# Output stores of an attention and gated-layers kernel: one store for each group of 32 tokens, issued in turn by SP and ACT

## The chip, the cores and the metric

The kernel runs on one core of a Trainium2 chip. The metric is the device time of one execution in microseconds (us). Traces come from one profiled execution, and times in them count from its first instruction.

## The reference

What is computed, cut to what matters: a Nystrom attention over 4 batches of 8 heads, 576 tokens and 64 values per head, and behind it two gated layers, whose result is the output.

```python
A, Bm, C = sm(q, k_lm), sm(q_lm, k_lm), sm(q_lm, k)     # 32 landmarks per head
# Z: six steps of an iterative pseudo-inverse of Bm
x = (A @ Z @ C @ v)            # to 2304 tokens x 512
x = ((silu(x @ w_gate1) * (x @ w_val1)) @ w_out1)        # d_ff = 1536
out = ((sigmoid(x @ w_gate2) * (x @ w_val2)) @ w_out2)   # 2304 x 512, f32
```

## The kernel before, in words

The attention's factors for each batch b are kept as A transposed (tile AH and its low part) and U = Z C v. The first layer works on U W1 (`uw_steps`): for each of six chunks c of 256 columns of d_ff, and each batch, eight matmuls, one for each head, form U W1 in eight tiles of 32 rows; the matmuls with A follow in `gv1_steps`. Those two functions stay as they are.

The stores belong to the second layer. Its tokens are kept in an order of their own: token number t in batch b is row 576 b + 18 t' + u of the output for t = 32 u + t', so that 32 neighbouring tokens on 32 partitions go to 32 output rows that lie 18 apart. Each row is 512 f32 numbers, 2 KB in one piece.

The second layer runs over d_ff in six chunks c (`NFC`) and in each over five chunks i of tokens: four of 512 tokens (one for each batch, `MT`), and a fifth of 256 tokens, the last 64 of each batch (`NR`). `gv2_steps(c, i)` has two halves ft: gate and value matmuls (tiles pg and pv), sigmoid on ACT (line 491), product on DVE (line 492), and a split into a high and a low part (ACT line 326, DVE line 327). `o2_steps(c, i)` takes 128 tokens at a time (t): six matmuls into a tile po, and DVE adds po to the tile oacc (line 513). In the last chunk (c = 5) the finished oacc tile is stored right behind its add: line 517 for the chunks of 512 tokens, one DMA for each tile of 128 tokens; line 520 for the fifth chunk, two DMAs for each tile. All are issued by SP.

The program interleaves by hand: the first half of the next `gv2_steps` is written ahead of `o2_steps` of the chunk at hand, the second half behind it. In c = 5 the order of the chunks is 0, 1, 2, 4, 3, so chunk 3 (512 tokens) ends the program, with no work behind its last adds but the stores.

The names DMAHW0 to DMAHW7 in the instruction lists are eight completion counters. The program's DMAs take them in turn, and a DMA waits until the DMA that last used its counter, eight DMAs earlier, has landed, unless something else already says so.

Of the kernel before, what the change touches and what calls it, by code (L numbers as in the profile page):

```python
# [14 lines left out]
def nystrom_moe_kernel(tc, q, k, v, wg1, wv1, wo1, wg2, wv2, wo2, out):  # L15
    nc = tc.nc
    B, H, S, D = q.shape
    M = 32
    P = 128
# [8 lines left out]
    MT = 512  # L28
# [14 lines left out]
    def ptile(shape, tag, name):  # L43
        return psum.tile(shape, F32, tag=tag, name=name, bufs=PB[tag])
# [16 lines left out]
    def mm(o, l, r, start=True, stop=True):  # L61
        nc.tensor.matmul(o, l, r, start=start, stop=stop, skip_group_check=True)  # L62
# [314 lines left out]
    def otag(layer, c):  # L377
        nps[0] += 1
        return "oa"[nps[0] % 2] if layer or c >= OA else "o"
# [85 lines left out]
    NR = S - MT  # L465
# [32 lines left out]
    def o2_steps(c, i):  # L498
        w = WO[1, c]
        for t in range(0, CHUNKS[i], P):  # L500
            if c == 0:
                OACC[i, t] = late["o"].tile([P, DM], F32, tag="oacc", name=f"oacc{i}_{t}", bufs=B * S // P)
            acc = OACC[i, t]
            ps = ptile([P, DM], otag(1, c), f"po2_{c}_{i}_{t}")
            n = 0
            for ft in range(2):
                for a, x in TERMS:
                    mm(ps, H2[c, i, ft][a][:, t:t + P], w[:, x, ft, :], start=(n == 0), stop=(n == 5))
                    n += 1
            if c == 0:  # L510
                nc.scalar.copy(acc, ps)
            else:
                nc.vector.tensor_tensor(acc, ps, acc, op=ALU.add)  # L513
            if c == NFC - 1:
                rows = out.rearrange("(b t u) d -> b u t d", b=B, u=L)
                if i < B:
                    nc.sync.dma_start(rows[i, t // M:(t + P) // M], acc)
                else:
                    for x in range(P // NR):
                        nc.sync.dma_start(rows[t // NR + x, MT // M:], acc[NR * x:NR * (x + 1), :])  # L520
            yield


# [81 lines left out]
    for i, (c, b) in enumerate(order):  # L605
        if c + 1 < NFC and b == 0:
            wfill.append(weights(1, c + 1))
        main(g2)
        if i + 1 < len(order):
            nc_, nb_ = order[i + 1]  # L610
            need(1, nc_, 3)
            g2 = gv2_steps(nc_, nb_)
            next(g2)
        need(1, c, 5)
        main(o2_steps(c, b))
# [38 lines left out]
```

## Time and profile before

| | us |
|---|---|
| median of 3 runs | 936.54 |
| lowest, highest | 935.5, 939.15 |
| profiled execution | 937.11 |
| its span, first to last instruction | 935.3 |

The profiled execution is 1.8 us longer than its span, and 0.6 us above the median. Granted TensorE clock over the span: 0.983 of full speed. A page of the profile gives the busy time of each engine, the span in 40 slices, the DMA queues, the chain of work that ended last, and the costliest groups of instructions; the trace behind it can be asked for the instructions of a stretch in order of time and for busy shares in short stretches (the DMA share is the mean over the core's 16 DMA engines).

### The profile page before, as it was taken

What the parts mean: (1) busy time and instruction counts of PE and PEld (TensorE: products, weight loads), DVE (VectorE), ACT (ScalarE), POOL (GpSimd) and SP (SyncE); (2) the same over time, 40 slices, a digit from 0 to 9 for tenths busy, and PEclk for the clock granted to TensorE, in tenths of its full rate; (3) what the DMA queues carried; (4) which work ended last, traced back from release to release, by engine and by line L of the source; (5) the groups of instructions that cost most, each with busy time, mean ns of one, the idle gap of its engine ahead of it and who ended that gap; (6) DMA issues with size and microseconds to landing.
All of it is one profiled execution on the core that took longest, in us unless ns stands there. A gap on an engine that the chain in (4) does not pass through costs nothing.

```text
span 935.3 us, 16158 instructions
## 1 busy us (share of the span) xinstructions
PE 896.4 (96%) x6664; PEld 746.8 (80%) x6664; DVE 549.2 (59%) x1165; ACT 389.7 (42%) x833; POOL 0.7 (0%) x6
## 2 busy tenths in 40 slices
PE   5689999999999999999999999999999999999994
PEld 4456866677989999998998888888888888888883
DVE  7789968647777668869962153455346247232331
ACT  6569745546636346537653262143124114111110
POOL 0000000000000000000000000000000000000000
PEclk9779999999999999999999999999999999999998
DMA  8664311003313103202110021012003000000121
GB/s 271 193 189 151 91 52 39 15 1 91 125 57 90 46 18 119 90 1 91 46 39 7 1 87 49 1 47 88 1 13 123 1 1 23 0 1 1 61 76 67
DMA packets 25617, 57.66 MB, mean 62 GB/s; under 512 B 2760, under 2 KB 5832, under 8 KB 25544
## 3 DMA queue, kind: packets, MB, share of 16 engines
q1 hardware_dynamic: 25544, 56.63, 19.3%
q8 instruction: 52, 0.85, 0.4%
q14 instruction: 21, 0.17, 0.1%
HBM read 51.90 MB, written 4.72 MB: 61 GB/s over the span
## 4 chain that ended last, share of the span: by engine, by line
PE 91%; DVE 5%; ACT 1%; DMA 1%; issue 1%; SPq 0%; ACTq 0%; DVEq 0%
PE po L62 33%; PE pg L62 24%; PE pv L62 23%; PE pu L62 3%; PE nw L62 2%; PE tp L121 2%; DVE lm L107 1%; DMA kin<-in_k_dram 1%; PE cs L62 1%; PE cv L62 1%; PE as L62 1%; PE lt L62 1%; PE et L207 1%; DVE hl L327 0%; DVE cv L295 0%
## 5 line engine op out<-in xcount | busy, mean ns | idle before, releaser
L62 PE MATMUL po<-hh,wo 128*128 128x288 f32 x768 | 162.9, 303 | 1.0 <-DVE uw L327 0.7
L62 PE MATMUL po<-wo,h 128*128 128x512 f32 x648 | 152.2, 390 | 0.0
L492 DVE TENSOR_TENSOR hf<-hf,pv 128x512 f32<-128x512 f32 (+1 forms) x60 | 38.1, 634 | 194.2 <-PE pv L62 194.2
L62 PEld LDWEIGHTS po<-wo,h 128*128 128x128 f32 x648 | 121.1, 188 | 25.4 <-ACT h L326 0.3
L62 PEld LDWEIGHTS po<-hh,wo 128*128 128x128 f32 x768 | 123.0, 188 | 20.6 <-issue 13.7
L62 PE MATMUL pg<-AH,w 128*128 128x512 f32 (+1 forms) x480 | 136.2, 368 | 0.0
L62 PE MATMUL pv<-AH,w 128*128 128x512 f32 (+1 forms) x480 | 136.0, 368 | 0.0
L62 PE MATMUL po<-hl,wo 128*128 128x288 f32 x384 | 115.1, 300 | 0.3 <-DVE hl L327 0.3
L62 PE MATMUL pg<-AH,uw 128*128 128x288 f32 x576 | 98.9, 298 | 2.5 <-ACT uw L326 2.4
L491 ACT ACTIVATE hf<-pg 128x512 f32<-128x512 f32 (+1 forms) x60 | 33.1, 552 | 163.7 <-PE pg L62 163.0
L62 PEld LDWEIGHTS pg<-AH,w 128*128 128x128 f32 x480 | 87.3, 188 | 15.4
L62 PEld LDWEIGHTS pv<-AH,w 128*128 128x128 f32 x480 | 87.0, 189 | 15.0
L62 PE MATMUL pv<-AH,uw 128*128 128x288 f32 x576 | 95.9, 296 | 0.0
L62 PEld LDWEIGHTS pg<-AH,uw 128*128 128x128 f32 x576 | 83.2, 188 | 9.2 <-ACT uw L326 5.3
L326 ACT CAST h<-hf 128x512 fp32r<-128x512 f32 (+1 forms) x60 | 34.6, 576 | 125.6 <-DVE hf L492 125.6
L513 DVE TENSOR_TENSOR oacc<-po,oacc 128x512 f32<-128x512 f32 x90 | 61.9, 691 | 41.1 <-PE po L62 39.9
L62 PEld LDWEIGHTS pv<-AH,uw 128*128 128x128 f32 x576 | 82.6, 188 | 2.9 <-ACT sg L419 0.8
L62 PE MATMUL pg<-x1l,w 128*128 128x512 f32 x192 | 74.7, 389 | 0.0
L62 PE MATMUL pv<-x1l,w 128*128 128x512 f32 x192 | 74.7, 389 | 0.0
L62 PEld LDWEIGHTS po<-hl,wo 128*128 128x128 f32 x384 | 72.2, 188 | 2.7 <-issue 1.1
L447 DVE TENSOR_TENSOR acc<-po,acc 128x288 f32<-128x288 f32 x128 | 55.9, 454 | 16.8 <-PE po L62 16.0
L419 ACT ACTIVATE sg<-pg 128x288 f32<-128x288 f32 x96 | 39.1, 407 | 51.8 <-PE pg L62 51.2
(106 smaller groups left out, 1092.6 us busy)
## 6 DMA issues: line engine op xcount, KB each, us to landing
raw<-in_moe_w_out_dram SPq DMA_DIRECT2D x24, 512.0 KB
raw<-in_moe_w_gate_dram SPq DMA_DIRECT2D x36, 256.0 KB
raw<-in_moe_w_val_dram SPq DMA_DIRECT2D x36, 256.0 KB
kin<-in_k_dram SPq DMA_DIRECT2D x8, 576.0 KB
qin<-in_q_dram SPq DMA_DIRECT2D x8, 576.0 KB
vin<-in_v_dram SPq DMA_DIRECT2D x8, 576.0 KB
out_dram<-oacc SPq DMA_DIRECT2D x16, 256.0 KB
raw<-in_moe_w_gate_dram SPq DMA_DIRECT2D x24, 128.0 KB
```

Of the source, the lines that this page charges most:

```text
L62: nc.tensor.matmul(o, l, r, start=start, stop=stop, skip_group_check=True)
L107: nc.vector.tensor_reduce(lm, src.rearrange("p u d -> p d u"), axis=AX.X, op=ALU.add)
L121: nc.tensor.transpose(ps[:, j], flat(src[:, 2 * u:2 * u + 2]), ident)
L207: nc.tensor.transpose(ps[:, j, :], flat(e[:, r // 2, r % 2]), ident)
L326: nc.scalar.copy(hi, x)
L419: nc.scalar.activation(sg, pss[0], AF.Silu)
L447: nc.vector.tensor_tensor(sl, ps, sl, op=ALU.add)
L491: nc.scalar.activation(h, pss[0], AF.Sigmoid)
L492: nc.vector.tensor_tensor(h, h, pss[1], op=ALU.mult)
L513: nc.vector.tensor_tensor(acc, ps, acc, op=ALU.add)
```

## The change

In place of one store (or two) for each tile of 128 tokens there are four, each of 32 partitions by 512 f32 numbers (64 KB). The even ones are issued by SP, the odd ones by ACT.

```diff
             if c == NFC - 1:
+
                 rows = out.rearrange("(b t u) d -> b u t d", b=B, u=L)
-                if i < B:
-                    nc.sync.dma_start(rows[i, t // M:(t + P) // M], acc)
-                else:
-                    for x in range(P // NR):
-                        nc.sync.dma_start(rows[t // NR + x, MT // M:], acc[NR * x:NR * (x + 1), :])
+                for y in range(P // M):
+                    bb, u = (i, t // M + y) if i < B else ((t + M * y) // NR, (MT + (t + M * y) % NR) // M)
+                    eng = nc.scalar if y % 2 else nc.sync
+                    eng.dma_start(rows[bb, u], acc[M * y:M * y + M, :])
             yield
```

The same rows and bytes are written. The instructions of PE, DVE and POOL keep their order; ACT gets 36 DMAs and SP has 36 in place of 20.

On ACT, in the last chunk of d_ff, the first place is between the split of one half (line 326) and the sigmoid of the next (line 491). Before (h and hf are the tiles of the gated product, the numbers 5_1 are c and i):

```order
L491 ACTIVATE hf_5_0_9510<-pg_5_0_9484 128x512 [waits PE_49,Activation_49]
L326 CAST h_5_0_9513<-hf_5_0_9510 128x512 [waits DVE_49]
L491 ACTIVATE hf_5_1_9543<-pg_5_1_9517 128x512 [waits PE_49,Activation_49]
L326 CAST h_5_1_9546<-hf_5_1_9543 128x512 [waits DVE_49]
L491 ACTIVATE hf_5_1_9612<-pg_5_1_9586 128x512 [waits PE_49,Activation_49]
L326 CAST h_5_1_9615<-hf_5_1_9612 128x512 [waits DVE_49]
```

The same place in the changed kernel:

```order
L326 CAST h_5_1_9546<-hf_5_1_9543 128x512 [waits DVE_49]
L520 DMA out_dram<-oacc_0_6848 32x512 [waits DVE_49]
L520 DMA out_dram<-oacc_0_6848 32x512
L520 DMA out_dram<-oacc_128_6860 32x512 [waits DVE_49]
L520 DMA out_dram<-oacc_128_6860 32x512
L520 DMA out_dram<-oacc_256_6877 32x512 [waits DMAHW0_49,DVE_49]
L520 DMA out_dram<-oacc_256_6877 32x512 [waits DMAHW2_49]
L520 DMA out_dram<-oacc_384_6889 32x512 [waits DMAHW4_49,DVE_49]
L520 DMA out_dram<-oacc_384_6889 32x512 [waits DMAHW6_49]
L491 ACTIVATE hf_5_1_9624<-pg_5_1_9598 128x512 [waits PE_49,Activation_49]
```

Eight DMAs of chunk 0's output now stand ahead of the sigmoid of chunk 1's second half, and they wait for the adds on DVE and for earlier stores.

On SP the other place is the end of the program: the stores of the fifth chunk (oacc_0_7315, oacc_128_7324) and of chunk 3, four tiles of 128 tokens. Before:

```order
L520 DMA out_dram<-oacc_0_7315 2x32x512 [waits DMAHW4_49,DVE_49]
L520 DMA out_dram<-oacc_0_7315 2x32x512 [waits DMAHW5_49]
L520 DMA out_dram<-oacc_128_7324 2x32x512 [waits DMAHW6_49,DVE_49]
L520 DMA out_dram<-oacc_128_7324 2x32x512 [waits DMAHW7_49]
L517 DMA out_dram<-oacc_0_7213 4x32x512 [waits DMAHW0_49,DVE_49]
L517 DMA out_dram<-oacc_128_7222 4x32x512 [waits DMAHW1_49,DVE_49]
L517 DMA out_dram<-oacc_256_7231 4x32x512 [waits DMAHW2_49,DVE_49]
L517 DMA out_dram<-oacc_384_7240 4x32x512 [waits DMAHW3_49,DVE_49]
L649 UNCONDITIONAL_BRANCH
```

In the changed kernel the same end, from the fifth chunk's second tile on:

```order
L520 DMA out_dram<-oacc_128_7324 32x512 [waits DMAHW5_49,DVE_49]
L520 DMA out_dram<-oacc_128_7324 32x512 [waits DMAHW7_49]
L520 DMA out_dram<-oacc_0_7213 32x512 [waits DMAHW1_49,DVE_49]
L520 DMA out_dram<-oacc_0_7213 32x512 [waits DMAHW3_49]
L520 DMA out_dram<-oacc_128_7222 32x512 [waits DMAHW5_49,DVE_49]
L520 DMA out_dram<-oacc_128_7222 32x512 [waits DMAHW7_49]
L520 DMA out_dram<-oacc_256_7231 32x512 [waits DMAHW1_49,DVE_49]
L520 DMA out_dram<-oacc_256_7231 32x512 [waits DMAHW3_49]
L520 DMA out_dram<-oacc_384_7240 32x512 [waits DMAHW5_49,DVE_49]
L520 DMA out_dram<-oacc_384_7240 32x512 [waits DMAHW7_49]
L649 UNCONDITIONAL_BRANCH
```

SP has the odd counters now and ACT the even ones, so that a store waits for the fourth one before it on its own engine: that of the tile two back.

## Rows read from the trace of the kernel before

**Rows 1.** Busy time of each engine over the span, from the page.

```profile
PE 896.4 (96%) x6664; PEld 746.8 (80%) x6664; DVE 549.2 (59%) x1165; ACT 389.7 (42%) x833; POOL 0.7 (0%) x6
```

**Rows 2.** Stretches: busy us (instructions) by engine, granted clock, DMA share, GB/s.

```profile
862.00:922.30 60.30, 59.60 (x285) 49.56 (x283) 22.03 (x34) 8.29 (x15) 0.00 (x0) 1.00 0.18 61
922.30:935.30 13.00, 0.00 (x0) 0.00 (x0) 0.03 (x1) 0.00 (x0) 0.00 (x0) 0.67 0.22 83
```

**Rows 3.** Instructions of DVE and SP at the end, in order of time.

```profile
918.87 1.29 DVE L513 TENSOR_TENSOR oacc<-po,oacc 128x512 f32<-128x512 f32 x2 [0.83 <-PE po L62]
920.26 0.69 DVE L513 TENSOR_TENSOR oacc<-po,oacc 128x512 f32<-128x512 f32 x1
921.63 0.69 DVE L513 TENSOR_TENSOR oacc<-po,oacc 128x512 f32<-128x512 f32 x1 [0.68 <-PE po L62]
...
919.59 4.04 SPq L517 DMA_DIRECT2D out_dram<-oacc  x4
...
922.35 1.27 SPq L517 DMA_DIRECT2D out_dram<-oacc  x1
```

**Rows 4.** What SP's queue waited for: us in total, times, longest.

```profile
SPq L649 <- DMA out_dram<-oacc: 10.6, 1, 10.6
```

**Rows 5.** Short stretches at the end, columns as in rows 2.

```profile
914.00:916.00 2.00, 2.00 (x11) 1.65 (x10) 0.03 (x1) 0.00 (x0) 0.00 (x0) 1.00 0.13 46
...
932.20:932.60 0.40, 0.00 (x0) 0.00 (x0) 0.00 (x0) 0.00 (x0) 0.00 (x0) 0.50 0.26 102
...
933.80:934.20 0.40, 0.00 (x0) 0.00 (x0) 0.00 (x0) 0.00 (x0) 0.00 (x0) 0.50 0.03 10
```

**Rows 6.** SP's issues of stores: duration ns min/median/max, first and last start.

```profile
L517 SPq DMA_DIRECT2D out_dram<-oacc x16: 527/537/1274, 865.9 to 922.4; - x16
L520 SPq DMA_DIRECT2D out_dram<-oacc x4: 511/528/716, 909.8 to 911.7; - x4
```

**Rows 7.** The start of chunk 1's stores: issue on SP, and short stretches.

```profile
882.26 0.53 SPq L517 DMA_DIRECT2D out_dram<-oacc  x1
...
882.80:883.20 0.40, 0.40 (x4) 0.32 (x3) 0.33 (x2) 0.00 (x0) 0.00 (x0) 1.00 0.00 0
883.20:883.60 0.40, 0.40 (x3) 0.33 (x2) 0.39 (x1) 0.00 (x0) 0.00 (x0) 1.00 0.14 31
883.60:884.00 0.40, 0.40 (x3) 0.35 (x2) 0.00 (x0) 0.00 (x0) 0.00 (x0) 1.00 0.40 31
884.00:884.40 0.40, 0.40 (x3) 0.32 (x3) 0.14 (x1) 0.00 (x0) 0.00 (x0) 1.00 0.39 15
884.40:884.80 0.40, 0.40 (x4) 0.32 (x3) 0.40 (x1) 0.00 (x0) 0.00 (x0) 1.00 0.05 5
```

**Rows 8.** A train of four weight loads of 128 KB (64 rows each), last issue and end.

```profile
300.93 0.60 SPq L314 DMA_DIRECT2D raw<-in_moe_w_val_dram  x1
...
301.50:302.00 0.50, 0.50 (x12) 0.34 (x18) 0.50 (x2) 0.50 (x3) 0.00 (x0) 1.00 0.78 217
302.50:303.00 0.50, 0.50 (x17) 0.09 (x1) 0.11 (x1) 0.50 (x2) 0.00 (x0) 1.00 0.62 209
303.00:303.50 0.50, 0.50 (x4) 0.50 (x5) 0.39 (x1) 0.50 (x2) 0.00 (x0) 1.00 0.01 4
```

**Rows 9.** ACT and PE around chunk 0's and chunk 1's stores and at the end.

```profile
872.08 0.60 ACT L491 ACTIVATE hf<-pg 128x512 f32<-128x512 f32 x1 [6.81 <-PE pg L62]
888.40 0.60 ACT L491 ACTIVATE hf<-pg 128x512 f32<-128x512 f32 x1 [6.81 <-PE pg L62]
891.85 0.62 ACT L326 CAST h<-hf 128x512 fp32r<-128x512 f32 x1 [2.86 <-DVE hf L492]
893.73 5.63 PE L62 MATMUL po<-wo,h 128*128 128x512 f32 x24
...
869.30 0.69 DVE L513 TENSOR_TENSOR oacc<-po,oacc 128x512 f32<-128x512 f32 x1 [0.67 <-PE po L62]
913.24 0.60 ACT L491 ACTIVATE hf<-pg 128x512 f32<-128x512 f32 x1 [4.09 <-PE pg L62]
915.97 0.69 DVE L492 TENSOR_TENSOR hf<-hf,pv 128x512 f32<-128x512 f32 x1 [4.82 <-PE pv L62]
```

## The prediction

> **What bounds the kernel now.** I read the page's busy times first: PE is busy for 896.4 of 935.3 us [rows 1]. A change of stores can gain nothing there unless PE waits for one, and no matmul reads what a store writes. So I looked for a stretch in which PE is idle, and the stretches show one: until 922.3 us PE is busy for 59.6 of 60.3 us, and from 922.3 to the end, 13.0 us, no engine computes while the DMA engines run at a share of 0.22 [rows 2]. The reader is to see there that these 13 us are a tail of stores.
>
> The instructions at the end say the same: the last add ends at 921.63 + 0.69 = 922.32, SP issues the last store at 922.35 and is through at 923.62 [rows 3]. Then it waits 10.6 us for the stores to land [rows 4], that is to 934.2, and the last 1.1 us are the end of the program.
>
> What makes the tail long is the rate. While it lasts the DMA share is 0.26 and 102 GB/s flow: 4 of the 16 DMA engines work, at 25 GB/s each [rows 5]. From 914 to 916, where only the fifth chunk's stores are under way, the share is 0.13 at 46 GB/s, 2 engines [rows 5]. The stores' outermost sizes are 4 (4x32x512, line 517) and 2 (2x32x512, line 520). Chunk 3's 1 MB takes 10 us at 102 GB/s, and it starts behind what the fifth chunk's 512 KB left on two of those four engines. Elsewhere more engines work: in a train of loads of 64 rows the share is 0.62 to 0.78, 10 to 12 engines' worth on average, at 209 to 217 GB/s [rows 8].
>
> **The change, part by part.** PE, DVE and POOL keep their order, so until 922.32 nothing should move unless ACT is late (below). What remains is when the last of the new stores lands.
>
> *Rate.* A store is now 32 rows of 2 KB. I take it that its 32 rows go to all 16 engines, two rows each, as those of the 64-row loads go to more than four. Even at the loads' 209 GB/s a tile of 256 KB then needs 1.25 us in place of 2.6, and the 512 KB of the fifth chunk is gone long before chunk 3's first store. The Trainium skill's page "DMA: Bandwidth & Descriptors" (section "Why a DMA increments its semaphore by 16 and not by 1") says that a DMA uses the largest number of engines up to 16 that divides the slowest size of both sides. By that the old stores use 4 and 2, which rows 5 bear out, and the new ones would use 16, which no row here shows.
>
> *Issue.* SP's issues of stores last 0.53 us (median), 0.51 at least; the longest, 1.27 us, is the last one, behind the backlog [rows 6]. I take 0.53 for SP and, lacking any row of an ACT issue, for ACT too. Each engine has two for each tile, side by side with the other.
>
> *Landing time L, from the start of an issue until the counter says so.* From issue to first packet: the issue at 882.26 moves nothing until 883.2 and little before 883.6, about 1.15 us [rows 7]. From last packet to the end of the wait: packets end near 934.0, the wait at 934.2, so 0.2. Between: at full pace two rows of 2 KB on an engine at 25 GB/s take 0.16 us, hence a lower bound L = 1.5. But the first packets of a burst of stores are slow: from 883.2 to 884.8 only 0.4 x (31 + 31 + 15 + 5) = 33 KB pass [rows 7]. If a store of 64 KB pays this start of 1.6 us in full, L = 2.95; if the pair from SP and ACT pay it one after the other, L = 4.55, the upper bound. For small loads the train's last issue starts at 300.93 and its packets are over at about 303.0 [rows 8]: 2.1 + 0.2 gives 2.3. I take L = 2.6, between 2.3 and 2.95.
>
> *The new wait.* A store waits for the fourth one before it on its engine. In the last chunk the adds end at 919.56, about 920.16, 920.95 and 922.32 [rows 3]: the first three tiles come faster than 2 issues of 0.53 allow, so SP's four issues for tiles 0 and 1 start at 919.59, 920.12, 920.65 and 921.18. The third tile's first store must wait for the first tile's to land, 919.59 + L, and so on; the fourth tile's second store starts at 921.18 + L (from L = 2.1 on; below, the issues themselves set it, at 923.30). It lands L later. ACT runs beside it in the same steps.
>
> *Sum.* End of the span = 921.18 + 2 L + 1.1 = 922.28 + 2 L. With L = 2.6 that is 927.5, against 935.3: **7.8 us less**. The bounds: L = 1.5 gives 923.30 + 1.5 + 1.1 = 925.9, 9.4 us less; L = 4.55 gives 931.4, 3.9 us less. Without the wait on the counters the last store would start at 922.88, and the gain with L = 2.6 would be 8.7: the wait gives back about 0.9.
>
> *What is costed at nothing.* SP's 16 more issues: it has nothing else to do there. ACT's 36 issues, 19 us at 0.53, in a stretch where ACT is busy for 8.3 of 60.3 us [rows 2]. They hold up what stands behind them on ACT, which is the sigmoid of the next half. After chunk 0 the last add ends at 869.99 and ACT's two issues are done by 871.1, the sigmoid starts at 872.08 when its matmuls end [rows 9]: covered by 1 us, and by more, since the product also waits for pv. At the program's last sigmoid, 913.24, the fifth chunk's adds (last one done at about 911.15) leave 1 us too, and another 2.1 until the product's own wait for pv ends at 915.97 [rows 9].
>
> Against the profiled execution's 937.11 us this makes 929.3. The median of the runs is 0.57 lower, so for a median I expect 936.54 - 7.8 = 928.7; I give 928.8.
>
> **Rivals.**
>
> *The stores land late.* The queue is then held by its own counters. For: the slow start in rows 7, which 64 KB stores meet more often than 256 KB ones. Against: the loads of 128 KB in rows 8 don't show it. Each us of L costs 2 us at the end. At L = 4.16 the gain falls to 4.7 us, 0.5%, and beyond it the change reads as none: 931.9 to 933.
>
> *The rate stays.* If the small stores still run at 102 GB/s in all, on few engines or one after the other, chunk 3's 1 MB starts at 919.59 + 1.15, pays 1.6, needs 10.1, and the span ends near 933.7: 1.6 us less, time 934.9, no change. For: 32 rows are on the SBUF side a quarter of the partitions, and no row shows such a store. Against: the number of engines follows the outermost size in rows 5. The same page of the Trainium skill ("Rules for kernel authors") advises one transfer on 128 partitions over several on parts of them, since these serialize on the same engines. By that rule this rival holds; it speaks of transfers that have all engines already, which rows 5 show these have not.
>
> *ACT becomes the bound (slower).* If an ACT issue, with its wait, costs c, the eight issues of a chunk hold the next sigmoid. The tightest full chunk is chunk 1: first issue at about 882.3; the next chunk's matmuls need the split of the half behind it at 893.73 + 0.68 = 894.4 (after three matmuls of 0.227), the chain from the start of the sigmoid to the end of the split is 1.96, so the sigmoid may start at 892.45 in place of 888.40 [rows 9]: 10.2 us for 8 issues, c = 1.27. The others bite at 1.6, 1.4 and, for the last four, 1.4. Beyond, lateness is about 28 c - 39.5 us. To undo 7.8 us and lose 4.7 more takes 12.5, so c = 1.86, three and a half times SP's median: 941.3 us and up. Against: even SP's longest issue was 1.27, behind a backlog that would be gone.
>
> **How the numbers follow.** The likeliest case, L from 1.5 to 3.3, 926.9 to 930.3 us: 0.80. Stores that land late: 0.09, of which 0.06 still gain over 0.5% and 0.03 don't. Rate stays: 0.06. ACT the bound, or landing so late that it costs: 0.05. What a measurement of this kernel can tell from no change is 0.5%, 4.7 us. So faster 0.80 + 0.06 = 0.86, same 0.03 + 0.06 = 0.09, slower 0.05. The range runs from the lower bound, 926.5 with some spread of the runs, to 932.3, which takes in most of the late landings.
>
> **What would show it.** In the changed profile: DMA share in bursts of over 0.5 after each add in place of a steady 0.26; the add that ends near 922.3 as before; the tail about 5 us in place of 13; SP and ACT stores of chunk 3's third and fourth tile that wait for a DMA, not for DVE; ACT's issues about 0.53 us; the sigmoids at 872, 888 and 913 where they were. Wrong would be: a share that stays near 0.26 in the tail, a last add later than 922.5, or an ACT issue above 1.2 us.

## The result, and the profile after

The changed kernel takes 926.53 us (median; 925.59 to 927.86), the kernel before beside it 937.25 us: a ratio of 0.9894, 95% interval 0.9879 to 0.991. It is faster by 1%, some 10 us. Two more comparisons of the same kernel, below, gave 0.9895 (0.988 to 0.9911) and 0.9906 (0.989 to 0.9923).

First the stretches of the changed kernel, cut at the end of its last add (columns as in [rows 2]).

```profile
862.00:919.76 57.76, 57.03 (x273) 47.47 (x271) 21.42 (x34) 8.29 (x15) 0.00 (x0) 1.00 0.30 73
919.76:923.80 4.04, 0.00 (x0) 0.00 (x0) 0.00 (x0) 0.00 (x0) 0.00 (x0) 1.00 0.53 145
```

The tail in which no engine computes is 4.04 us, where it was 12.98 (from 922.32 to 935.3, [rows 2, 3]): 8.9 us less. Its DMA share is 0.53 at 145 GB/s, where it was 0.22. The span is shorter by 11.5 us; the other 2.6 lie before the last add, and the repeats below show what they are.

Then the last instructions of DVE, SP and ACT in order of time, which answer to [rows 3].

```profile
916.30 2.08 DVE L513 TENSOR_TENSOR oacc<-po,oacc 128x512 f32<-128x512 f32 x3 [0.82 <-PE po L62]
917.03 4.28 SPq L520 DMA_DIRECT2D out_dram<-oacc  x8
917.03 4.51 ACTq L520 DMA_DIRECT2D out_dram<-oacc  x8
919.07 0.69 DVE L513 TENSOR_TENSOR oacc<-po,oacc 128x512 f32<-128x512 f32 x1 [0.68 <-PE po L62]
```

SP and ACT issue side by side, eight stores each, and the last of them start after the last add has ended at 919.76. Issues near the end, SP's and ACT's (the first line holds two):

```profile
917.90 0.84 SPq L520 DMA_DIRECT2D out_dram<-oacc  x2
...
920.41 0.32 SPq L520 DMA_DIRECT2D out_dram<-oacc  x1
920.77 0.54 SPq L520 DMA_DIRECT2D out_dram<-oacc  x1
918.25 0.37 ACTq L520 DMA_DIRECT2D out_dram<-oacc  x1
918.66 0.43 ACTq L520 DMA_DIRECT2D out_dram<-oacc  x1
920.60 0.32 ACTq L520 DMA_DIRECT2D out_dram<-oacc  x1
921.22 0.32 ACTq L520 DMA_DIRECT2D out_dram<-oacc  x1
```

The fourth tile's sum is ready at 919.76, but SP starts its first store at 920.41 and ACT at 920.60 and 921.22. Each is the fourth after another on its engine: 920.41 follows 917.90 by 2.51, 920.60 follows 918.25 by 2.35, 921.22 follows 918.66 by 2.56 us. That is the wait on the eight counters. In SP's list of waits it is one of the two in the second line, 0.5 us of the 1.4; the longer one, 0.8, ends at 899.9, when SP's next store is far off, and costs nothing. The first line is the end of the program, which waited 10.6 us before [rows 4]:

```profile
SPq L649 <- DMA out_dram<-oacc: 1.5, 3, 0.6
SPq L520 <- DMA out_dram<-oacc: 1.4, 2, 0.8
```

The stores' issues (duration ns min/median/max, first and last start) and their landing times, which answer to [rows 6]:

```profile
L520 SPq DMA_DIRECT2D out_dram<-oacc x36: 314/395/1176, 863.4 to 920.8; - x36
L520 ACTq DMA_DIRECT2D out_dram<-oacc x36: 321/432/1536, 863.4 to 921.2; - x36
...
DMA to landing us min/median/max: 1.6/2.0/3.9
```

Short stretches of the tail, for [rows 5]: the share is about 1 where it was 0.26, and it ends 2.7 us after the last add.

```profile
918.00:918.40 0.40, 0.40 (x3) 0.34 (x2) 0.39 (x1) 0.00 (x0) 0.00 (x0) 1.00 1.05 220
...
919.60:920.00 0.40, 0.00 (x0) 0.00 (x0) 0.16 (x1) 0.00 (x0) 0.00 (x0) 1.00 0.99 302
...
922.40:922.80 0.40, 0.00 (x0) 0.00 (x0) 0.00 (x0) 0.00 (x0) 0.00 (x0) 1.00 0.08 21
```

And the sigmoids on ACT that now stand behind stores, for [rows 9]:

```profile
869.52 0.60 ACT L491 ACTIVATE hf<-pg 128x512 f32<-128x512 f32 x1 [6.81 <-PE pg L62]
...
885.85 0.60 ACT L491 ACTIVATE hf<-pg 128x512 f32<-128x512 f32 x1 [6.81 <-PE pg L62]
...
899.69 0.38 ACT L491 ACTIVATE hf<-pg 128x256 f32<-128x256 f32 x1 [7.38 <-PE pv L62]
...
910.68 0.60 ACT L491 ACTIVATE hf<-pg 128x512 f32<-128x512 f32 x1 [4.09 <-PE pg L62]
```

The third of them in the kernel before:

```profile
900.89 0.38 ACT L491 ACTIVATE hf<-pg 128x256 f32<-128x256 f32 x1 [6.03 <-PE pg L62]
```

With the 2.56 us by which everything lies earlier, three of the four stand where they stood. The one at 899.69 is 1.36 us late (900.89 - 2.56 would be 898.33). An ACT issue of 1.54 us, the longest, ran ahead of it, from 897.57 on, with one more issue between the two. PE lost nothing by it: up to the end of the last add it idles 0.7 us, 57.76 - 57.03, as before, 60.3 - 59.6 [rows 2].

### The profile page after: what moved, and what is told of

The parts are those of the page before. It is cut to its first block, busy times and chain, and to the rows that moved or that the text cites. A ratio compares the mean times of both kernels' runs of the same rounds, so it can differ in the third digit from the quotient of the medians.

```text
span 923.8 us, 16229 instructions
## 1 busy us (share of the span) xinstructions
PE 896.7 (97%) x6664; PEld 747.5 (81%) x6664; DVE 549.0 (59%) x1165; ACT 389.3 (42%) x833; POOL 0.7 (0%) x6
## 4 chain that ended last, share of the span: by engine, by line
PE 91%; DVE 5%; ACT 2%; DMA 1%; issue 1%; SPq 0%; DVEq 0%; ACTq 0%
PE po L62 33%; PE pg L62 24%; PE pv L62 24%; PE pu L62 3%; PE nw L62 2%; PE tp L121 2%; DVE lm L107 1%; PE cs L62 1%; DMA kin<-in_k_dram 1%; PE cv L62 1%; PE as L62 1%; PE et L207 1%; PE lt L62 0%; DVE hl L327 0%; DVE cv L295 0%
## 5 line engine op out<-in xcount | busy, mean ns | idle before, releaser
L62 PE MATMUL po<-wo,h 128*128 128x512 f32 x648 | 152.2, 390 | 0.0
L62 PEld LDWEIGHTS po<-hh,wo 128*128 128x128 f32 x768 | 123.2, 188 | 20.5 <-issue 13.7
```

## The experiments

Theories. **Engines**: a store's outermost size sets how many DMA engines work on it (4 or 2 before, 16 for 32 rows), and the whole gain is the shorter tail. **Queues**: two issuing engines bring the rate. **Split**: small stores land sooner, whatever their shape. Beside them the question of what the 2.6 us ahead of the last add are.

**The changed kernel once more** (no edit).

> The changed kernel once more, to see what of its gain is the tail and what is the spread of the first stages, whose code did not change. Theory (all of the gain is the tail after the last add: 13.0 us before, 4.0 after): ratio 0.990 to 0.991, a tail of 4.0 us again, and the last add's end anywhere within about 3 us of 922.3. Rival (the change also moves the stages before, by 2.5 us as in the first pair of traces): ratio 0.988, last add's end near 919.8 again.

Ratio 0.9895 (0.988 to 0.9911), just below the 0.990 expected. The tail of its trace:

```profile
923.70:927.70 4.00, 0.00 (x0) 0.00 (x0) 0.00 (x0) 0.00 (x0) 0.00 (x0) 0.80 0.53 149
```

The tail is 4.0 us again, but the last add ends at 923.7, 1.4 us later than in the kernel before and 3.9 later than in the first trace of the same kernel. A third trace, run later beside two other kernels, had it at 920.7.

> The changed kernel beside the two others on the same chip: ratio 0.989 to 0.991, tail 4.0 us; the last add's end somewhere between 919 and 924.

Ratio 0.9906 (0.989 to 0.9923), tail 4.0. The spread is there long before any store: the first copy of line 445 starts at 91.6 us in the kernel before, and at 89.2, 93.1 and 90.1 in the three traces of the changed one. From that copy to the end of the last add all four take 830.6 to 830.7 us. So the 2.6 us ahead of the last add are spread of the first stages, not the change, and the rival falls.

**All stores issued by SP.**

```diff
-                    eng = nc.scalar if y % 2 else nc.sync
+                    eng = nc.sync
```

> The same 72 stores of 32 rows, all issued by SP. Theory (the engines come from the 32 rows of a store, the second issuing queue only saves issue time): the DMA share goes over 0.5 in bursts as with both queues; the last four tiles' 16 issues of 0.42 us take 6.7 us, so the last one starts 6.3 us after the first, lands 2.0 later, and the tail is 6.5 us in place of 4.0: ratio 0.992 to 0.994. Rival (two queues bring the rate): the tail stays near 13 us, ratio 1.0.

930.0 us, ratio 0.994 (0.9927 to 0.9952). In order of time, SP's last stores; then a stretch of the tail:

```profile
918.23 7.56 SPq L520 DMA_DIRECT2D out_dram<-oacc  x16
```

```profile
921.00:926.00 5.00, 0.00 (x0) 0.00 (x0) 0.00 (x0) 0.00 (x0) 0.00 (x0) 0.92 0.58 141
```

Sixteen issues take 7.56 us, 0.47 each, and 64 KB every 0.47 us are the 141 GB/s that flow: issuing is the bound. The tail is 6.94 us. So one queue alone gives two thirds of the gain in the tail (6.0 of 8.9 us), and the second queue the rest, by issuing in parallel.

**The old stores, issued in turn by SP and ACT.**

```diff
-                    nc.sync.dma_start(rows[i, t // M:(t + P) // M], acc)
+                    (nc.scalar if (t // P) % 2 else nc.sync).dma_start(rows[i, t // M:(t + P) // M], acc)
```

The fifth chunk's stores alternate in the same way.

> The stores of before (4x32x512 and 2x32x512), issued in turn by SP and ACT. Theory (a store's outermost size says how many engines work, and both queues use the same ones): DMA share stays 0.26 in the tail, tail 12 to 13 us, ratio 0.998 to 1.002. Rival (two queues bring the rate): share 0.5 and a tail of 6 to 8 us, ratio 0.993 to 0.995.

936.76 us, ratio 1.001 (1.0001 to 1.0019). In the tail:

```profile
926.00:931.00 5.00, 0.00 (x0) 0.00 (x0) 0.00 (x0) 0.00 (x0) 0.00 (x0) 0.50 0.26 91
```

The share stays 0.26: both queues' stores of outermost size 4 go to the same four engines. The tail is 13.7 us (last add's end at 921.14, span 934.8), a little above the 12 to 13 expected. A second queue brings no rate.

**Two stores of 64 tokens for each tile.**

```diff
-                for y in range(P // M):
-                    bb, u = (i, t // M + y) if i < B else ((t + M * y) // NR, (MT + (t + M * y) % NR) // M)
+                for y in range(P // NR):
+                    bb, u = (i, t // M + 2 * y) if i < B else (t // NR + y, MT // M)
                     eng = nc.scalar if y % 2 else nc.sync
-                    eng.dma_start(rows[bb, u], acc[M * y:M * y + M, :])
+                    eng.dma_start(rows[bb, u:u + 2], acc[NR * y:NR * y + NR, :])
```

> Two stores of 2x32x512 for each tile of 128 tokens, SP and ACT in turn: a split too, but with 2 as the outermost size. Theory: share 0.13, 46 to 51 GB/s all the way, so that 4.72 MB need 94 us from 867 on and the span ends near 963: time about 965, ratio 1.03; the sigmoids late in the last two chunks because ACT waits for stores on the eight counters. Rival (splitting or two queues is what helps): a tail of 4 to 8 us, ratio 0.99 to 0.995.

964.26 us, ratio 1.0305 (1.029 to 1.032). Stretches of it, and ACT's instructions around the fifth chunk's sigmoid:

```profile
870.00:890.00 20.00, 20.00 (x95) 16.77 (x94) 5.43 (x8) 2.44 (x4) 0.00 (x0) 1.00 0.13 52
...
930.10:961.40 31.30, 0.00 (x0) 0.00 (x0) 0.01 (x1) 0.00 (x0) 0.00 (x0) 0.57 0.12 48
```

```profile
896.60 16.50 ACTq L520 DMA_DIRECT2D out_dram<-oacc  x4
913.21 0.38 ACT L491 ACTIVATE hf<-pg 128x256 f32<-128x256 f32 x1 [17.70 <-issue]
```

Share 0.13 and 52 GB/s: two engines, on either queue. A split with 2 as the outermost size is 3% slower, which takes the theory of the split away. It also shows the prediction's slower rival at work. ACT's four stores stretch over 16.5 us, the sigmoid behind them waits 17.7 us, PE stalls, and the last add ends at 930.1.

**One store for each tile, to rows that follow one another** (the output's rows come in another order).

```diff
-                    nc.sync.dma_start(rows[i, t // M:(t + P) // M], acc)
+                    nc.sync.dma_start(out[S * i + t:S * i + t + P, :], acc)
```

In the fifth chunk two stores of 64 rows each, likewise.

> One store for each tile of 128 tokens, issued by SP as before, but to 128 rows in a row (64 in the fifth chunk), so that its outermost size is 128 on both sides; the output's rows come in another order for it. Theory (the engines are all of it, the split is not needed): share over 0.5 in bursts, no store waits for a counter, the last store starts right behind the last add and lands 2.0 to 2.6 us later, tail 3.1 to 3.7 us, ratio 0.989 to 0.990. Rival (the split into small stores is what helps, landing being quicker for 64 KB): tail 5 us or more, ratio 0.992 or more.

925.85 us, ratio 0.9886 (0.9873 to 0.99). The last issue; then a stretch with stores under way, and the tail:

```profile
920.12 0.33 SPq L516 DMA_DIRECT2D out_dram<-oacc  x1
```

```profile
918.50:919.30 0.80, 0.80 (x4) 0.38 (x2) 0.23 (x1) 0.00 (x0) 0.00 (x0) 1.00 1.03 379
...
920.10:923.30 3.20, 0.00 (x0) 0.00 (x0) 0.00 (x0) 0.00 (x0) 0.00 (x0) 1.00 0.29 106
```

No split and no second queue, as before the change, only an outermost size of 128: the share is about 1, and the tail is 3.2 us, 0.8 shorter than the change's. The last store starts with the add's end, where the change's last one starts 1.46 us behind it. The ratio cannot tell the two apart.

**All stores issued by ACT.**

```diff
-                    eng = nc.scalar if y % 2 else nc.sync
+                    eng = nc.scalar
```

> The 72 stores of 32 rows, all issued by ACT: 16 issues ahead of a sigmoid in place of 8. By the bound of the prediction (10.2 us for a chunk's issues until PE is late) 16 issues of 0.43 us, 6.9 us, cost PE nothing: last add's end within the spread of the others, tail 6.5 us as with SP alone, ratio 0.992 to 0.994. Rival (issues on ACT hold up the sigmoids to PE's cost): PE gaps ahead of po in chunks 1 and 2 and a last add 2 us or more later, ratio 0.996 or more.

931.29 us, ratio 0.9944 (0.9932 to 0.9957), just above what was expected. On ACT, behind chunk 0:

```profile
863.87 7.56 ACTq L520 DMA_DIRECT2D out_dram<-oacc  x16
871.53 0.60 ACT L491 ACTIVATE hf<-pg 128x512 f32<-128x512 f32 x1 [8.33 <-DMA out_dram<-oacc]
```

Sixteen issues last 7.56 us, the sigmoid waits for them, and PE does not. The tail is 7.9 us, 1.4 more than expected and 0.9 more than with SP alone. That 0.9 is not ACT's issuing: from the first of the last sixteen stores to the last of them it takes 7.06 us on ACT and 7.14 on SP, but the fourth of the last chunk's adds ends 1.80 us after the first in place of 2.75, so that more of the issuing lies behind it. The last split lies about 0.5 us later than in the kernel with plain rows, measured from DVE's split at the head of the last chunk's adds (52.02 against 51.52 us). But here the order that PE works in changed too in a few places, and from the first copy of line 445 to the last add's end it takes 831.4 us in place of 830.7, so whether ACT costs that half microsecond stays open.

**One store for each tile in the right order**, in three ways. Tokens reordered where the product is split into two parts, by strided writes (hp are views of the two parts):

```diff
-            split(hl[0][:, 0:n_t], hl[1][:, 0:n_t], h)
+            nu = P // M if i < B else NR // M
+            hp = [x[:, 0:n_t].rearrange("p (k t u) -> p k u t", u=nu, t=M) for x in hl]
+            split(hp[0], hp[1], h.rearrange("p (k u t) -> p k u t", u=nu, t=M))
...
-                    nc.sync.dma_start(rows[i, t // M:(t + P) // M], acc)
+                    nc.sync.dma_start(rows[i, :, t // M:(t + P) // M], acc)
```

with rows as "b t u d" and the fifth chunk's two stores likewise.

> The output as it should be and one store for each tile: the second layer's product is written to its two parts with the 32 neighbouring tokens outermost (token, then group), so that a tile's 128 partitions go to 32x4x512 of the output, 32 as the outermost size, four rows (8 KB) in one piece, issued by SP alone. If strided writes cost ACT and DVE nothing: tail 3.1 to 3.7 us, ratio 0.989. If they double the last split's 1.3 us: 1.3 us later, ratio 0.990 to 0.991. If packets of 8 KB or the order slow the store: tail 5 us or more.

927.27 us, ratio 0.9904 (0.9889 to 0.9919). The last split on ACT and DVE, and DVE's part of it in the kernel before (ACT's takes 0.62 there, as in [rows 9]):

```profile
915.00 1.10 ACT L326 CAST h<-hf 128x512 fp32r<-128x512 f32 x1 [2.85 <-DVE hf L492]
916.12 1.09 DVE L327 TENSOR_TENSOR h<-hf,h 128x512 fp32r<-128x512 f32 x1 [1.16 <-ACT h L326]
...
917.34 0.69 DVE L327 TENSOR_TENSOR h<-hf,h 128x512 fp32r<-128x512 f32 x1 [0.69 <-ACT h L326]
```

The tail is 3.5 us, but the split takes 1.10 and 1.09 us in place of 0.62 and 0.69, which at the program's end nothing covers: from the first copy of line 445 to the last add's end it takes 831.6 us, 0.9 more than in the kernel before. What the tail wins over the change's 4.0 us, the split gives back.

The same with strided reads (the parts as "p k t u", the product read in that order):

> As the kernel with the tokens reordered in the split (one store of 32x4x512 for a tile), but the two parts are written in one piece and the product is read with a stride. If the cost of 0.48 us on ACT and 0.40 on DVE that the strided writes had lies in the writing: the split back at 0.62 and 0.69, tail 3.5 us, ratio 0.989. If any access with a stride costs it: split at 1.1 and 1.1 again, ratio 0.990 to 0.991.

928.42 us, ratio 0.9911 (0.9895 to 0.9926): the split takes 1.10 and 1.09 us again, and the tail is 3.5 us. On which side the stride lies makes no difference here.

A tile of every fourth token, so that nothing changes on ACT and DVE:

```diff
-                    mm(ps, H2[c, i, ft][a][:, t:t + P], w[:, x, ft, :], start=(n == 0), stop=(n == 5))
+                    mm(ps, H2[c, i, ft][a][:, (slice(t // P, MT, MT // P) if i < B else slice(t, t + P))], w[:, x, ft, :], start=(n == 0), stop=(n == 5))
...
-                    nc.sync.dma_start(rows[i, t // M:(t + P) // M], acc)
+                    nc.sync.dma_start(rows[i, 0:MT // M, t // P::MT // P], acc)
```

Here rows stays "b u t d", as before; the fifth chunk stores 32 rows at a time, all from SP.

> A tile of 128 tokens takes every fourth token of its chunk in place of 128 neighbours: the weight loads of the second layer's output matmuls step by four numbers, nothing on ACT or DVE changes, and the store goes to 16x8x512 of the output, 16 as the outermost size, one DMA on SP (the fifth chunk in stores of 32 rows, SP alone). Theory: full share, no wait for counters, tail 3.2 to 3.7 us, ratio 0.988 to 0.990 if the stepped weight loads cost nothing. Rival: stepped weight loads take longer than the 0.227 us of a matmul, and then the 648 of them add 0.1 us or more each in the second layer: 65 us or more slower.

933.02 us, ratio 0.9959 (0.9944 to 0.9975). The group of its weight loads, then the same in the kernel before (busy us, mean ns):

```profile
L62 PEld LDWEIGHTS po<-wo,h 128*128 128x128 f32 x648 | 150.7, 296 | 3.7 <-ACT h L326 0.2
...
L62 PEld LDWEIGHTS po<-wo,h 128*128 128x128 f32 x648 | 121.1, 188 | 25.4 <-ACT h L326 0.3 <-DVE h L327 0.2
```

One stretch with its last stores under way:

```profile
926.40:928.40 2.00, 0.02 (x1) 0.00 (x0) 0.69 (x1) 0.00 (x0) 0.00 (x0) 1.00 0.90 313
```

One store of 128 partitions from one queue, with one row of 2 KB and the next lying apart in the output as before the change, but with 16 in place of 4 as the outermost size: the share is 0.90. So the engines do not come from writing the rows in one piece. The tail is 3.8 us (3.2 to 3.7 expected). But the 648 weight loads are busy for 150.7 us in place of 121.1, 0.233 for each in place of 0.187, just above the 0.227 of a matmul, and the weight loads' idle time falls from 25.4 to 3.7 us: they seem to be hidden behind the matmuls no longer. The matmuls of that group are busy 157.5 us in place of 152.2, and these 5.3 us, of the 5.5 by which the last add ends later as counted from the first copy of line 445, are most of what the tail had won. The rival's 0.1 us for each was far too much.

## Why the prediction was right, point by point

*The tail bounds, nothing else moves.* Right: PE's busy time is the same (896.4 and 896.7 us), and in three traces of the changed kernel the last add's end is spread over 919.8 to 923.7, around the 922.3 of before. The 923.7 is later than 922.5, which I had named as a sign of being wrong, but it comes from the first stages: counted from the first copy of line 445 nothing moved.

*Rate.* Right: share about 1.0 in place of 0.26. The outermost size as the cause is shown by four kernels: stores of 4 on two queues (0.26), of 2 (0.13), and single stores of 16 (0.90, tail 3.8 us) and of 128 (about 1, tail 3.2 us). The Trainium skill's rule on the number of engines, in the page "DMA: Bandwidth & Descriptors" (section "Why a DMA increments its semaphore by 16 and not by 1"), agrees with all of them. Its other advice there ("Rules for kernel authors"), one transfer on 128 partitions in place of two on halves of them, would have spoken against the change. Here it is borne out between stores that use all engines: one plain store has the shorter tail (3.2 against 4.0 us).

*Issue.* 0.40 (SP) and 0.43 (ACT) in place of 0.53, side by side. Kernels with one issuer show what this is worth: a tail of 6.9 or 7.9 us.

*Landing time.* The mis-sized term. I took L = 2.6 us for every store; the median is 2.0. It stands in the sum twice. The first time it was right: the last store starts 2.56 us after the one that holds it up. The last store itself landed in 1.7: issued at 921.22, it leaves 0.9 us to the span's end at 923.8, where I had put 1.1 for the end of the program. The sum 922.28 + 2 L put the tail at 5.2 us; 4.0 was measured, 0.9 of the difference from the last landing and 0.2 from the program's end, so the tail gained 8.9 us and not 7.8.

That 2.6 was right the first time is in part luck. I had worked it out from the slow start in rows 7, which the new stores do not pay in full: most landed in 1.6 to 2.1 us. There are two moments at which they took longer. Landing times of the stores that start from 863 to 895.7, from 896.2 to 899.05, and from 917.88 to 919.9:

```profile
DMA to landing us min/median/max: 1.6/1.9/2.1
...
DMA to landing us min/median/max: 2.9/3.7/3.9
...
DMA to landing us min/median/max: 2.1/2.4/2.5
```

In both moments a single packet of a queue that the profile calls "instruction" moves too (packets, MB, share of 16 engines, from 897.2 to 898.8 and from 918.95 to 919.75):

```profile
q8 instruction: 1, 0.02, 5.6%
...
q14 instruction: 1, 0.01, 5.2%
```

Both repeats show late landings and such a packet at the same two places of the program. Whether the packet holds the stores up is not shown. In the last chunk the first three adds also end only 0.6 and 0.8 us apart, so that the bunched stores are a second explanation, and no run separates the two. (The kernel with plain rows has adds as close and no such packet there, and its last stores land in 2.0 to 2.1 us, as those of its first two chunks do; but it has four stores where this one has sixteen.)

*The new wait.* Right on where the last store starts: 1.46 us after the add, as the sum has it (921.18 + 2.6 - 922.32). Too large in what the wait costs: ACT was still issuing the third tile's stores until 920.29, so without the wait its last one would have started near 920.7 (an estimate, from issues of 0.32 to 0.37 us), and the wait gives back some 0.5 us where 0.9 was predicted. And I had the third tile's stores wait too. They did not: SP's first one starts at 918.84, 1.8 us after the first tile's and not 2.6, right behind the issue ahead of it, because the first tile's stores had landed in 1.6 to 2.0.

*ACT.* Right on the cost, nothing; not on the length. One ACT issue in the first trace lasted 1.54 us, above the 1.2 that I had named as a sign of being wrong. It came singly (the repeats' longest are 1.00 and 1.32), and the bound of 1.27 to 1.6 us was for each of eight.

*The number.* 928.8 was forecast and 926.5 measured in the first comparison. The tail's extra 1.1 us is half of that difference; the rest is within the interval (8.4 to 11.3 us of gain). My range began at 926.5, so the measured median lies at its edge, and of the repeats' medians 926.11 lies below it and 927.64 inside: which side of the edge a median falls on is chance. (By the sum, L from 1.5 to 3.3 gives 927.1 to 930.1; the 926.9 to 930.3 that I gave for it is 0.2 wider at each end.) The three comparisons gave gains of 10.7, 9.5 and 8.9 us, the tail 8.9.

## What to carry to other kernels

When a kernel ends with a stretch in which no engine computes and the DMA share stands at a plain fraction such as 0.25 or 0.125, look at the outermost size of the stores on both sides: it sets how many of the 16 engines work. Here 2 and 4 gave two and four engines, and 16, 32 and 128 gave nearly all or all of them. Change it if that costs the compute engines nothing; a split into several stores is one way, and it brings its own issues, and waits on completion counters. A gain of this kind is at most the tail, and the tail is read from one trace more exactly than from the times.

## What the runs showed of the hardware that was not expected

- A cast or subtraction of 128x512 f32 that writes with a step of four numbers, or reads groups of four with a step of 32, takes 1.1 us in place of 0.62 (ACT) and 0.69 (DVE). On the fifth chunk's 128x256, where the groups are of two, the same writes take 0.42 (ACT) and 0.43 (DVE) in place of 0.41 and 0.42, the same reads 0.47 and 0.43.
- Weight loads that step by four numbers keep the loader busy for 0.233 us each in place of 0.187.
- A 256 KB store to rows in a row is issued in 0.33 us, to 4x32x512 in 0.54, to 32x512 (64 KB) mostly in 0.31 to 0.54. Landing takes 2.0 to 2.1 us for the first in the last chunk, 2.4 for 32x4x512, 2.9 for 16x8x512.
- The few long issues on SP and ACT (1.18 and 1.54 us in the first trace, from 897.57 to 899.11) fall at the place of the program where stores landed in 2.9 to 3.9 us. The repeats have them at the same place (up to 1.00 and 1.32 us). The packet of the queue "instruction" shown above moves at the same time; whether it is the cause stays open.
